# Threshold attention and a feed-forward block on one core: later weights, attention first on two engines, split scores from job three, a margin in the order

## The chip, the core and the metric

The kernel runs on one core of one Trainium2 chip. The metric is the device time of one execution in microseconds (us). The core has five engines that run side by side, each through its own list of instructions in order: PE (TensorE, the matrix multiplier; its weight loads are shown as PEld), DVE (VectorE), ACT (ScalarE), POOL (GpSimd) and SP (SyncE, which here issues every DMA). SBUF is the working memory, PSUM the memory that PE writes.

## The reference

For 8 batches, 8 heads, 576 positions and 64 values a head, attention keeps of each row of scores only those within `tau` of the row's largest, and takes a softmax over them. Its output, 8 x 576 x 512, goes through a feed-forward block (FFN) in which each position is mixed with the one before it, twice (`xk` and `xr`).

```python
scores = scale * np.matmul(q, k.transpose(0, 1, 3, 2))
thresh = np.max(scores, axis=-1, keepdims=True) - tau
scores = np.where(scores >= thresh, scores, -1000000000.0)
scores = scores - np.max(scores, axis=-1, keepdims=True)
attn = np.exp(scores)
attn = attn / (np.sum(attn, axis=-1, keepdims=True) + 1e-09)
x = np.matmul(attn, v)                    # then (B, S, H * D) = (8, 576, 512)
...
xk = mu_k * x + (1.0 - mu_k) * x_prev
xr = mu_r * x + (1.0 - mu_r) * x_prev
k = np.maximum(xk @ w_k, 0.0)             # w_k 512 x 1024
v = k * k @ w_v                           # w_v 1024 x 512
r = 1.0 / (1.0 + np.exp(-(xr @ w_r)))     # w_r 512 x 512
return (r * v).astype(np.float32)
```

The three weight matrices come as float64.

## The kernel before

**Planned order.** The program is not written in the order in which it runs. Each piece of work is a `Step`, added to a `Plan` with its engine, an estimate of how long it occupies it (`occ`), what it reads and writes, and a `key` (a small key goes first). `Plan.order` then goes through time with these estimates: it takes, over all engines, the step that could start first (ties by key), gives it its buffer, and so makes a list, in which the steps are issued. The chip runs each engine's part of this list in that order. So a changed estimate or key moves instructions on every engine. PSUM has two kinds of tile: `s` (two of them, scores of one head for 128 queries) and `w` (four, everything else).

**Jobs and units.** A job is a pair of heads of one batch; here jobs are counted from one. Most have five units: a tail `T` of 64 queries and four blocks `P` of 128 queries. Batch one is done in two halves, so that the first FFN chunk can start early: jobs one to four have two blocks each, jobs five to eight two blocks and the tail. A block has two halves `y`, one for each head.

**A block's way.** Scores on PE into `s` (L498 or L509); DVE takes the row maximum (L543); ACT shifts it by tau (L551) and takes the exponential into `p` (L559); DVE sets to zero what lies under the threshold and sums the row (L567), and inverts the sum (L577, L578); POOL scales the row (L592); PE transposes it in blocks of 128 (L617), ACT or DVE copies these from PSUM to `pm` and `pl` (L629, L631; DVE takes one of the two only where the block's number is above `EARLY`). After two blocks `attend` multiplies them with v (L690, L693), and DVE copies the result to `xT` (and the tail to `xE`).

**Two ways to score.** The first `PLAIN` = 8 jobs multiply in float32 straight from `raw` (L498), one step that fills both `s` tiles. The others split each operand into a high part `hi` (ACT, L422) and a rest `lo` (POOL, L428, two instructions a job), lay them out in `st` tiles by eight DMAs a job (L447; there are three pairs of `st` tiles, a job uses two), and score each half by a step of its own (L509, the tail L484).

**Weights.** The 20 weight tiles (8 of `w_k`, 4 of `w_r`, 8 of `w_v`) are fetched as 64-bit words (L331) and turned into numbers: ACT takes the absolute value of the high word (L340), DVE four steps (L348, L362, L369, L379), ACT makes the high part (L386), POOL the rest (L390). `xT` of the second batch serves as scratch for this. The plan lets the j-th fetch start at W0 + W1 * j = 3 + 3.5 j of its own time.

**FFN chunks.** A chunk is 256 positions: POOL takes the difference of neighbours (L777), DVE the mix (L786), ACT and POOL split it (L799, L807). Then PE multiplies with `w_k` (L829), ACT takes relu, square and high part (L837, L838, L842), POOL the rest (L852); PE multiplies with `w_r` (L871) and `w_v` (L893), each product as three matmuls of split operands; the sigmoid is ACT's (L879), the last product DVE's (L899). There are 18 chunks: two a batch, and one for the tails of every four batches. The first chunk needs jobs one to four. Steps of chunks may fill in anywhere behind their key.

## Time and profile before

| what | value |
| --- | --- |
| median of three runs | 1138.61 us (1138.51 to 1140.61) |
| the profiled execution | 1139.91 us, span of the profile 1137.8 us |
| busy, share of the span | PE 92%, DVE 68%, ACT 64%, POOL 49% |
| granted TensorE clock, mean | 0.968 |

A profile row gives line, engine, operation, out<-in by the program's names, partitions x elements, and the count. In groups, busy time and mean duration (ns) follow, then the idle time of that engine just before them and what ended most of it. Times of PE are modelled at their ends: matmuls overlap, so starts are what to read. A rise of one engine's busy time costs nothing where it is not waited for.

### The profile page before, as it was taken

To read this page: it belongs to the slowest core of one execution; us is meant where nothing else is said; L and a number is where in the kernel's file an instruction comes from. 1 tells how busy PE (TensorE), PEld (TensorE's weight loads), DVE (VectorE), ACT (ScalarE), POOL (GpSimd) and SP (SyncE) were. 2 spreads that over 40 slices of the span, in tenths; PEclk is the share of its full clock that TensorE was granted. 3 is DMA by queue.
4 is the path that set the end of the run, shared out by engine and by line. 5 is a ranking of instruction groups with operands and counts; after the bars stand their busy time and mean duration, and the time that the engine had idled before them with its cause. 6 is when DMAs were issued, how large, how long until landed. Compare 5 with 4: busy or idle time off the path is not lost.

```text
span 1137.8 us, 19250 instructions
## 1 busy us (share of the span) xinstructions
PE 1047.7 (92%) x6840; PEld 850.9 (75%) x6840; DVE 770.0 (68%) x1703; ACT 725.4 (64%) x1532; POOL 554.7 (49%) x570
## 2 busy tenths in 40 slices
PE   5557988997999999999999999999999999999998
PEld 3335757875878778787877878787787878688887
DVE  6999457778777777778767777778877677611120
ACT  5565677766777757677674767777576667444443
POOL 2656335634654536456444644545454544444441
PEclk8767998999999999999999999999999999999999
DMA  6530154445525336254523534344543341000000
GB/s 236 195 127 35 46 161 105 110 100 122 132 61 146 80 97 150 61 121 100 143 53 94 123 95 117 81 109 99 137 110 91 75 92 38 10 23 25 19 19 19
DMA packets 36798, 106.76 MB, mean 94 GB/s; under 512 B 5984, under 2 KB 5984, under 8 KB 36704
## 3 DMA queue, kind: packets, MB, share of 16 engines
q1 hardware_dynamic: 36704, 105.54, 36.1%
q8 instruction: 55, 0.90, 0.3%
q14 instruction: 39, 0.32, 0.1%
HBM read 44.70 MB, written 9.44 MB: 48 GB/s over the span
## 4 chain that ended last, share of the span: by engine, by line
PE 62%; DVE 20%; ACT 9%; POOL 3%; issue 3%; DMA 2%; SPq 1%; POOLq 0%; DVEq 0%; ACTq 0%
PE w L829 14%; PE w L893 11%; PE w L617 10%; PE s L509 8%; PE w L690 8%; PE w L871 6%; DVE p L567 5%; DVE mk L786 5%; DVE sm L543 3%; ACT p L559 2%; PE w L693 2%; DVE sm L577 2%; POOL p L592 2%; PE s L484 2%; PE s L498 1%
## 5 line engine op out<-in xcount | busy, mean ns | idle before, releaser
L592 POOL TENSOR_SCALAR p<-p,sm 128x576 f32<-128x576 f32 x288 | 220.9, 779 | 287.9 <-DVE sm L578 195.5
L567 DVE SCALAR_TENSOR_TENSOR p<-s,sm,p 128x576 f32<-128x576 f32 x288 | 232.5, 814 | 96.9 <-ACT p L559 93.6
L543 DVE TENSOR_REDUCE sm<-s 128x1 f32<-128x576 f32 x288 | 210.9, 751 | 47.3 <-PE s L509 29.2
L829 PE MATMUL w<-xk,wk 128*128 128x256 f32 x1728 | 235.0, 285 | 0.2 <-ACT pm L629 0.2
L617 PE MATMUL w<-ident,p 128*128 128x128 f32 x1312 | 200.8, 285 | 25.9 <-POOL p L592 23.2
L893 PE MATMUL w<-wv,k 128*128 128x512 f32 x864 | 221.4, 397 | 1.1 <-DVE sg L899 0.9
L829 PEld LDWEIGHTS w<-xk,wk 128*128 128x128 f32 x1728 | 218.1, 190 | 2.0 <-issue 0.8
L617 PEld LDWEIGHTS w<-ident,p 128*128 128x128 f32 x1312 | 153.6, 145 | 77.2 <-POOL p L592 54.6
L559 ACT ACTIVATE p<-s,sm 128x576 f32<-128x576 f32 x288 | 209.9, 732 | 0.5
L893 PEld LDWEIGHTS w<-wv,k 128*128 128x128 f32 x864 | 155.6, 188 | 30.1 <-issue 1.2
L629 ACT ACTIVATE pm<-w 128x512 f32<-128x512 f32 x178 | 105.2, 592 | 110.3 <-PE w L617 109.7
L551 ACT ACTIVATE sm<-sm,small 128x1 f32<-128x1 f32 x288 | 83.7, 291 | 108.1 <-DVE sm L543 106.7
L690 PE MATMUL w<-pm,v 128*64 128x256 f32 (+1 forms) x1024 | 146.8, 426 | 4.9 <-DVE pm L631 2.7
L852 POOL TENSOR_TENSOR k<-r,k 128x512 fp32r<-128x512 f32 x72 | 93.3, 1296 | 85.4 <-ACT k L842 79.8
L786 DVE SCALAR_TENSOR_TENSOR mk<-m,mu_sb,xT 128x256 f32<-128x256 f32 x128 | 79.6, 662 | 80.7 <-POOL xk L807 80.4
L807 POOL TENSOR_TENSOR xk<-mk,xk 128x512 fp32r<-128x512 f32 x72 | 93.3, 1296 | 70.0 <-ACT xk L799 66.7
L690 PEld LDWEIGHTS w<-pm,v 128*64 128x64 f32 x1024 | 74.8, 142 | 59.6 <-issue 11.1
L509 PE MATMUL s<-st 128*128 128x288 f32 x448 | 106.3, 319 | 13.9 <-DVE p L567 7.3
L871 PE MATMUL w<-wr,xk 128*128 128x512 f32 x432 | 111.4, 397 | 0.0
L428 POOL TENSOR_TENSOR lo<-raw,hi 128x576 fp32r<-128x576 f32 (+1 forms) x56 | 83.6, 1509 | 56.5 <-ACT hi L422 46.3
L509 PE MATMUL s<-st,st 128*128 128x288 f32 x448 | 99.4, 304 | 0.0
L509 PEld LDWEIGHTS s<-st 128*128 128x128 f32 x448 | 72.6, 193 | 34.7 <-issue 17.0
(62 smaller groups left out, 1140.9 us busy)
## 6 DMA issues: line engine op xcount, KB each, us to landing
raw<-in_qk SPq DMA_DIRECT2D x36, 608.0 KB, 4.8
st<-hi SPq DMA_DIRECT2D x56, 304.0 KB, 3.3
st<-lo SPq DMA_DIRECT2D x56, 304.0 KB, 4.3
v<-in_v SPq DMA_DIRECT2D x36, 320.0 KB, 3.0
out<-sg SPq DMA_DIRECT2D x32, 256.0 KB, 2.0
st<-hi SPq DMA_DIRECT2D x56, 144.0 KB, 3.4
st<-lo SPq DMA_DIRECT2D x56, 144.0 KB, 3.7
wk<-in_w_k SPq DMA_DIRECT2D x8, 512.0 KB, 7.1
```

What stands on the lines that cost most here:

```text
L509: PE.matmul(ss[y].get()[:, z, 0:HS], l.get()[:, c * P : (c + 1) * P], r.get()[:, keys(y, z)], start=(j == 0), stop=(j == 1),)
L543: lambda sv=sv, col=col: V.tensor_reduce(col(0), sv(), axis=AX.XY, op=ALU.max, negate=True),
L559: lambda sv=sv, pv=pv, col=col: A.activation(pv(), sv(), AF.Exp, bias=col(0)),
L567: lambda sv=sv, pv=pv, col=col: V.scalar_tensor_tensor(pv(), sv(), col(1), pv(), op0=ALU.is_ge, op1=ALU.mult, accum_out=col(2)),
L592: lambda y=y: G.tensor_scalar(p.get()[:, y], p.get()[:, y], sm.get()[:, 3, y : y + 1], 0.0, op0=ALU.mult, op1=ALU.add),
L617: lambda c=c, o=o: PE.transpose(pt.get()[:, c, :], p.get().rearrange("p y s -> p (y s)")[:, o : o + P], ident.get()),
L629: fn = lambda: A.activation(out_(), in_(), AF.Copy)
L690: PE.matmul(o.get()[hs, 0:n], vt.get()[:, c, hs], pm.get()[:, h, c, 0:n], start=(c == 0), stop=False)
L786: V.scalar_tensor_tensor(d.get()[:, y, o : o + n], diff.get()[:, y, o : o + n], mu_sb.get()[:, j, hc + y : hc + y + 1], prv[:, hc + y], op ...
L829: PE.matmul(h.get()[:, f], l, r, start=(ct == 0 and i == 0), stop=(ct == NCT - 1 and i == 2))
L871: PE.matmul(z.get(), l, r, start=(ct == 0 and i == 0), stop=(ct == NCT - 1 and i == 2))
L893: PE.matmul(vps.get(), l, r, start=(ft == 0 and i == 0), stop=(ft == NFT - 1 and i == 2))
```

## The change

- `w_r` and `w_v` may be fetched in the plan only from 50 + 2 (j - 8) on, for the j-th tile; `w_k` as before.
- `soft`: DVE's and ACT's steps of the weights and of FFN chunks stand back. In the choice among an engine's steps they count as if they could start 0.3 later; the engine may so be kept for a step of attention that is ready a little later.
- `LATE`: from 150 of the plan's time on, PE's attention steps (those with key under -500) count as ready 0.3 later than their inputs are.
- `PLAIN` is 2: jobs three to eight use split scores.
- `EARLY` is 16 instead of 40: from job five on DVE takes one of the two `pm` copies.
- the four transposes of a half are one step; `attend` of the first units is five steps, one for each block of keys; keys of early `attend` move by 4.5 instead of 1.5.
- a second buffer for `r` (relu), and other estimates for some steps.

```diff
-    HOP = 0.05
+    HOP, LATE, FROM = 0.05, 0.3, 150.0
+    SOFT = {"DVE": 0.3, "ACT": 0.3}
...
+        s.soft = self.SOFT.get(eng, 0.0) if self.soft else 0.0
...
-                    k = (t, s.key, i)
+                    k = (t + s.soft, s.key, i, t)
...
-                n.ready = max(n.ready, t + s.occ if same else s.end + self.HOP)
+                late = self.LATE if n.eng == "PE" and n.key < -500 and t > self.FROM else 0.0
+                n.ready = max(n.ready, t + s.occ if same else s.end + self.HOP + late)
...
-    PREP, PB, VB, COLD, EARLY = 6, 2, 2, 24, 40
+    W0, W1, W2, W3, AVK = 3.0, 3.5, 50.0, 2.0, 4.5
+    PREP, PB, VB, COLD, EARLY = 6, 2, 2, 24, 16
...
-            wait=W0 + W1 * j,
+            wait=wait,
...
-                        0.104,
+                        0.26,
...
-        for c, o in enumerate(at):
-            add(
-                "PE",
-                0.109,
...
+        occ = 0.109 * len(at)
+        add(
+            "PE",
+            occ,
+            mm,
+            reads=[*((p, z) for z in y), ident],
+            writes=[pt, *to],
...
-        occ = 10 * 0.842e-3 * n + 0.2
-        if key < COLD:
-            occ *= 2
...
+        early = key < EARLY
+        for j, cs in enumerate([[0], [1], [2], [3], [4]] if early else [range(5)]):
+            occ = len(cs) * 1.66e-3 * n * (2 if key < COLD else 1) + (0.1 if early else 0.35)
...
-            r = sbuf("r", [P, 512], F32, 1)
+            r = sbuf("r", [P, 512], F32, 2)
...
-    PLAIN = 8
+    PLAIN = 2
...
-    W0, W1 = 3.0, 3.5
+    wfr = [W0 + W1 * j if j < 8 else W2 + W3 * (j - 8) for j in range(len(wlist))]
...
-                    attend(job, g, unit["n"] + 1.5)
+                    attend(job, g, unit["n"] + (AVK if unit["n"] < 20 else 1.5))
```

What this does to the order is shown at three places. A row is line, operation, out<-in and shape, with the matmuls of one group merged (x4); the number after a name tells tiles apart. Line numbers of the new kernel are 6 to 20 higher.

DVE, around the fourth block (the second of job two). Before, from behind this block's two reductions to the first of the next block:

```order
L379 SCALAR_TENSOR_TENSOR xT_77<-wk_0_167,xT_77 128x512
L379 SCALAR_TENSOR_TENSOR xT_77<-wk_0_189,xT_77 128x512
L567 SCALAR_TENSOR_TENSOR p_292,sm_279<-s_257,sm_279,p_292 128x576
L567 SCALAR_TENSOR_TENSOR p_292,sm_279<-s_259,sm_279,p_292 128x576
L348 TENSOR_SCALAR xT_77<-xT_77 128x512
L577 TENSOR_SCALAR sm_279<-sm_279 128x2
L578 RECIPROCAL sm_279<-sm_279 128x2
L362 TENSOR_SCALAR xT_77<-xT_77 128x512
L348 TENSOR_SCALAR xT_77<-xT_77 128x512
L369 SCALAR_TENSOR_TENSOR xT_77<-wk_0_230,xT_77 128x512
L362 TENSOR_SCALAR xT_77<-xT_77 128x512
L543 TENSOR_REDUCE sm_323<-s_308 128x1
```

And now:

```order
L551 TENSOR_REDUCE sm_270<-s_248 128x1
L551 TENSOR_REDUCE sm_270<-s_250 128x1
L386 SCALAR_TENSOR_TENSOR xT_77<-wk_0_146,xT_77 128x512
L355 TENSOR_SCALAR xT_77<-xT_77 128x512
L575 SCALAR_TENSOR_TENSOR p_294,sm_270<-s_248,sm_270,p_294 128x576
L644 COPY xT_73<-w_222 128x256
L369 TENSOR_SCALAR xT_77<-xT_77 128x512
L551 TENSOR_REDUCE sm_311<-s_305 128x1
L575 SCALAR_TENSOR_TENSOR p_294,sm_270<-s_250,sm_270,p_294 128x576
L585 TENSOR_SCALAR sm_270<-sm_270 128x2
L586 RECIPROCAL sm_270<-sm_270 128x2
L575 SCALAR_TENSOR_TENSOR p_322,sm_311<-s_305,sm_311,p_322 128x576
```

`wk` are weight tiles, `xT_77` their scratch. Before, seven of the eleven steps between the reductions of this block and the next belong to weights; now three and a copy of `xT` stand there, and the first reduction of job three (`s_305`, split scores) stands ahead of the masking of this block's second half.

PE, where the first FFN matmul stands. Before:

```order
L498 MATMUL s_709<-raw_408 128x288
L498 MATMUL s_711<-raw_408 128x288
L498 MATMUL s_709<-raw_408 128x288
L498 MATMUL s_711<-raw_408 128x288
L617 MATMUL w_727<-ident,p_702 128x128 x4
L617 MATMUL w_734<-ident,p_702 128x128
L829 MATMUL w_736<-xk_428,wk_0_155 128x256 x3
L829 MATMUL w_736<-xk_428,wk_0_184 128x256 x3
L829 MATMUL w_736<-xk_428,wk_0_238 128x256 x3
L829 MATMUL w_736<-xk_428,wk_0_243 128x256 x3
L829 MATMUL w_736<-xk_428,wk_0_155 128x256 x3
L829 MATMUL w_736<-xk_428,wk_0_184 128x256 x3
```

And now:

```order
L517 MATMUL s_714<-st_2_514 128x288 x2
L517 MATMUL s_714<-st_2_514,st_2_520 128x288 x2
L624 MATMUL w_740<-ident,p_667 128x128 x4
L624 MATMUL w_747<-ident,p_667 128x128
L624 MATMUL w_764<-ident,p_730 128x128 x4
L624 MATMUL w_774<-ident,p_730 128x128 x4
L624 MATMUL w_782<-ident,p_730 128x128
L849 MATMUL w_786<-xk_522,wk_0_163 128x256 x3
L704 MATMUL w_791<-pm_708,v_543 64x320 x8
L704 MATMUL w_791<-pl_725,v_543 64x320 x2
L849 MATMUL w_786<-xk_522,wk_0_206 128x256 x3
L849 MATMUL w_786<-xk_522,wk_0_266 128x256 x3
```

The FFN's first product (`w_736`, `w_786`) stands behind the tail of job five before, and now behind that job's second block too, whose rows are `p_730`; job five's `attend` follows at once.

SP, from the fetch of job three's `raw` on. Before:

```order
L400 DMA raw_135<-in_qk 128x1216
L331 DMA wk_0_146<-in_w_k 128x512
L331 DMA wk_0_167<-in_w_k 128x512
L331 DMA wk_0_189<-in_w_k 128x512
L331 DMA wk_0_230<-in_w_k 128x512
L331 DMA wk_0_246<-in_w_k 128x512
L413 DMA v_254<-in_v 128x640
L400 DMA raw_276<-in_qk 128x1216
L331 DMA wr_0_284<-in_w_r 128x512
L331 DMA wr_0_303<-in_w_r 128x512
L331 DMA wr_0_328<-in_w_r 128x512
```

And now:

```order
L408 DMA raw_135<-in_qk 128x1216
L338 DMA wk_0_146<-in_w_k 128x512
L338 DMA wk_0_165<-in_w_k 128x512
L455 DMA st_0_183<-hi_177 64x1216
L455 DMA st_0_187<-hi_177 64x576
L455 DMA st_1_199<-hi_177 64x1216
L455 DMA st_1_212<-hi_177 64x576
L338 DMA wk_0_216<-in_w_k 128x512
L455 DMA st_0_187<-lo_195 64x576
L455 DMA st_1_212<-lo_195 64x576
L408 DMA raw_236<-in_qk 128x1216
L455 DMA st_0_183<-lo_195 64x1216
```

Five tiles of `w_k` were fetched in one go; now three of them stand behind transfers that wait for `hi` and `lo`, and `w_r` comes much later.

More of the change, by code (lines that the diff above doesn't have):

```diff
@@ L44 @@
         "eng", "occ", "lat", "fn", "key", "deps", "succ", "allocs", "idx", "missing", "ready",
-        "start", "end", "kb",
+        "start", "end", "kb", "soft",
     )
 class Plan:
-    HOP = 0.05
+    HOP, LATE, FROM = 0.05, 0.3, 150.0
+    SOFT = {"DVE": 0.3, "ACT": 0.3}
     def __init__(self):
@@ L58, in __init__ @@
         self.bufs = []
+        self.soft = False
     def buf(self, *a, **k):
@@ L167, in order @@
                 if pick is not None and (best is None or pick[0] < best[0]):
-                    best = (pick[0], e, pick[2])
+                    best = (pick[0], e, pick[2], pick[3])
             if best is None:
                 raise RuntimeError("the plan is stuck")
-            t, e, i = best
+            _, e, i, t = best
             s = steps[i]
@@ L315, in tile_threshold_attention_then_rwkv_ffn, with weight @@
     pieces = {}
-    def weight(j, name, w, c, f, key):
+    def weight(j, name, w, c, f, key, wait):
+        plan.soft = True
         tag = f"w{name}{c}{f}"
@@ L394, in weight @@
         )
+        plan.soft = False
     def operands(job, key):
@@ L612, in transposes, with mm @@
         pt = psum("w", [P, 4, P], 4)
-        for c, o in enumerate(at):
-            add(
-                "PE",
-                0.109,
-                lambda c=c, o=o: PE.transpose(
-                    pt.get()[:, c, :], p.get().rearrange("p y s -> p (y s)")[:, o : o + P], ident.get()
-                ),
-                reads=[*((p, z) for z in y), ident],
-                writes=[(pt, c), *(to if c == 0 else ())],
-                key=key - 1000,
-                lat=0.28,
-            )
+        def mm():
+            for c, o in enumerate(at):
+                PE.transpose(
+                    pt.get()[:, c, :], p.get().rearrange("p y s -> p (y s)")[:, o : o + P], ident.get()
+                )
+        occ = 0.109 * len(at)
[5 more added lines that the diff above has]
+            writes=[pt, *to],
+            key=key - 1000,
+            lat=occ + 0.18,
+        )
         return pt
@@ L668, in turn_last @@
                 "ACT",
-                0.13,
+                0.22,
                 pe,
@@ L683, in attend, with mm @@
         o = psum("w", [P, 512], 4)
-        def mm():
-            for c in range(4):
+        def mm(cs):
+            for c in cs:
                 for h in range(2):
                     hs = slice(h * D, (h + 1) * D)
-                    PE.matmul(o.get()[hs, 0:n], vt.get()[:, c, hs], pm.get()[:, h, c, 0:n], start=(c == 0), stop=False)
-            for h in range(2):
-                hs = slice(h * D, (h + 1) * D)
-                PE.matmul(o.get()[hs, 0:n], vt.get()[:, 4, hs], pl.get()[:, 0:n], start=False, stop=True)
-        occ = 10 * 0.842e-3 * n + 0.2
-        if key < COLD:
-            occ *= 2
-        free = [(x, (hp, g))] + ([(xE, (b % NE, hp))] if n > CH else [])
-        add("PE", occ, mm, reads=[vt, pm, pl], writes=[o, *free], key=key - 1000, lat=occ + 0.2)
+                    pt = pl.get() if c == 4 else pm.get()[:, h, c]
+                    PE.matmul(o.get()[hs, 0:n], vt.get()[:, c, hs], pt[:, 0:n], start=(c == 0), stop=(c == 4))
+        free = [(x, (hp, g))] + ([(xE, (b % NE, hp))] if n > CH else [])
+        early = key < EARLY
+        for j, cs in enumerate([[0], [1], [2], [3], [4]] if early else [range(5)]):
+            occ = len(cs) * 1.66e-3 * n * (2 if key < COLD else 1) + (0.1 if early else 0.35)
+            add(
+                "PE",
+                occ,
+                lambda cs=cs: mm(cs),
+                reads=[vt, pm, pl],
+                writes=[o, *(free if j == 0 else [])],
+                key=key - 1000,
+                lat=occ + 0.2,
+            )
         evict(
@@ L766, in ffn_chunk @@
         pool_tt = 1.17 if kind == "main" else NTB * 0.39
+        plan.soft = True
         mix = [sbuf("xk", [P, 2, NCT, CH], FR, 2) for _ in range(2)]
@@ L793, in scale @@
                             )
-                add("DVE", 0.7 if nseg == 1 else 1.04, scale, reads=[diff, mu_sb, *sr], writes=[d], key=key)
+                add("DVE", 0.8 if nseg == 1 else 1.57, scale, reads=[diff, mu_sb, *sr], writes=[d], key=key)
                 add(
@@ L913, in ffn_chunk @@
                 )
+        plan.soft = False
     halved = {0: ([0, 1], [2, "T", 3])}
-    PLAIN = 8
+    PLAIN = 2
     jobs = []
@@ L942, in tile_threshold_attention_then_rwkv_ffn @@
     for j, (name, w, c, f) in enumerate(wlist):
-        weight(j, name, w, c, f, wat[j])
+        weight(j, name, w, c, f, wat[j], wfr[j])
     for job in jobs:
```

## Prediction

> **What bounds the kernel now.** I read the busy time by stretches first. Columns: stretch, its length, then PE, weight loads, DVE, ACT and POOL busy (with instruction counts), granted clock, DMA share, GB/s.
>
> ```profile
> 0.00:105.00 105.00, 58.66 (x255) 37.88 (x255) 93.18 (x172) 58.94 (x115) 53.13 (x49) 0.76 0.43 155
> 105.00:181.00 76.00, 69.77 (x426) 51.23 (x425) 42.84 (x102) 51.28 (x111) 31.31 (x34) 0.95 0.37 103
> 181.00:300.00 119.00, 108.12 (x731) 86.94 (x733) 92.06 (x210) 81.41 (x183) 58.76 (x64) 0.96 0.44 105
> 300.00:1000.00 700.00, 677.94 (x4644) 556.41 (x4641) 517.99 (x1159) 477.78 (x1034) 357.95 (x377) 1.00 0.40 96
> 1000.00:1138.00 138.00, 133.18 (x793) 118.47 (x791) 23.92 (x64) 55.94 (x89) 53.51 (x49) 1.00 0.06 20
> ```
>
> The kernel has two regimes. Up to 105 us DVE is busy 93.2 of 105 us and TensorE only 58.7, at a clock of 0.76. From there on TensorE is the bound: it idles 6.2, 10.9, 22.1 and 4.8 us in the four later stretches, 44 in all, against 46 in the first 105. Then the timeline of TensorE, for the borders (start, duration, instruction):
>
> ```profile
> 104.87 4.61 PE L829 MATMUL w<-xk,wk 128*128 128x256 f32 x33
> ...
> 162.92 1.62 PE L893 MATMUL w<-wv,k 128*128 128x512 f32 x6
> ...
> 179.34 0.76 PE L617 MATMUL w<-ident,p 128*128 128x128 f32 x5
> ...
> 180.21 0.42 PE L509 MATMUL s<-st,st 128*128 128x288 f32 x2
> ```
>
> The first FFN matmul starts at 104.9: from here TensorE always has something to fill in. The first chunk ends at 164.5. The last two rows belong to job eight; I come back to them. Last, what DVE does before 105 (count, busy us, mean ns, idle before):
>
> ```profile
> L567 DVE SCALAR_TENSOR_TENSOR p<-s,sm,p 128x576 f32<-128x576 f32 x19 | 15.1, 813 | 2.0 <-ACT p L559 1.9
> L362 DVE TENSOR_SCALAR xT<-xT 128x512 uint32<-128x512 uint32 x20 | 13.8, 698 | 0.0
> L543 DVE TENSOR_REDUCE sm<-s 128x1 f32<-128x576 f32 x19 | 13.4, 745 | 6.1 <-PE s L498 6.1
> L348 DVE TENSOR_SCALAR xT<-xT 128x512 f32<-128x512 f32 x20 | 11.4, 584 | 0.0
> L369 DVE SCALAR_TENSOR_TENSOR xT<-wk,xT 128x512 uint32<-128x512 uint32 x8 | 7.5, 952 | 0.1
> L369 DVE SCALAR_TENSOR_TENSOR xT<-wv,xT 128x512 uint32<-128x512 uint32 x7 | 7.2, 1035 | 0.0
> L379 DVE SCALAR_TENSOR_TENSOR xT<-wv,xT 128x512 uint32<-128x512 uint32 x7 | 6.5, 933 | 0.0
> L379 DVE SCALAR_TENSOR_TENSOR xT<-wk,xT 128x512 uint32<-128x512 uint32 x8 | 5.4, 680 | 0.0
> L786 DVE SCALAR_TENSOR_TENSOR mk<-m,mu_sb,xT 128x256 f32<-128x256 f32 x8 | 4.8, 636 | 0.0
> L577 DVE TENSOR_SCALAR sm<-sm 128x2 f32<-128x2 f32 (+1 forms) x10 | 4.6, 462 | 0.0
> L369 DVE SCALAR_TENSOR_TENSOR xT<-wr,xT 128x512 uint32<-128x512 uint32 x4 | 4.0, 994 | 0.0
> L379 DVE SCALAR_TENSOR_TENSOR xT<-wr,xT 128x512 uint32<-128x512 uint32 x4 | 3.8, 950 | 0.0
> ```
>
> The eight weight rows (L348, L362, L369, L379) add to 59.6 us: decoding the weights is more than half of what bounds the first stage, and only w_k is needed for its end.
>
> **Stage one, to the first FFN matmul.** In the new order DVE has, ahead of the mix that releases this matmul, 10, 8, 8 and 8 of the four weight steps, all of w_k but two, where the trace has 20, 20, 19 and 19. At the means above 24.3 us stay (5.8, 5.6, 7.5, 5.4) and 35.3 go. But those means hold waiting; alone, the steps are short:
>
> ```profile
> 78.09 0.42 DVE L362 TENSOR_SCALAR xT<-xT 128x512 uint32<-128x512 uint32 x1
> ...
> 79.03 0.68 DVE L369 SCALAR_TENSOR_TENSOR xT<-wv,xT 128x512 uint32<-128x512 uint32 x1
> ```
>
> At these, 22 short and 22 long steps removed are 24.2 us. I take the middle, 29.7, since both kinds of row stand in the trace. Added are two reductions, two maskings and a small step (job five's second half now comes before the FFN's start): 3.6 us. So without new waits the stage ends at 104.9 - 29.7 + 3.6 = 78.8.
>
> New waits: jobs three to eight get split scores. The cost on TensorE is nothing:
>
> ```profile
> 76.97 1.24 PE L498 MATMUL s<-raw 64*128 64x288 f32 x8
> 82.82 3.04 PE L498 MATMUL s<-raw 64*128 64x288 f32 x8 [4.61 <-issue]
> ...
> 227.46 0.42 PE L509 MATMUL s<-st 128*128 128x288 f32 x2
> ...
> 228.51 1.54 PE L893 MATMUL w<-wv,k 128*128 128x512 f32 x6
> ```
>
> Plain scores of a unit take 1.24 us at full clock and 3.04 at the low one; the split ones 228.51 - 227.46 = 1.05, and each half needs only its own PSUM tile. The price is the operands: one ACT copy, two POOL subtractions and eight transfers for each job.
>
> ```profile
> L422 ACT ACTIVATE hi<-raw 128x1216 fp32r<-128x1216 f32 x6 | 7.3, 1221 | 4.1 <-PE s L484 2.5 <-DMA st<-lo 1.5
> L428 POOL TENSOR_TENSOR lo<-raw,hi 128x576 fp32r<-128x576 f32 (+1 forms) x12 | 17.7, 1491 | 11.4 <-ACT hi L422 11.4
> 156.85 3.24 SPq L447 DMA_DIRECT2D st<-lo  x4
> st<-lo SPq DMA_DIRECT2D x56, 304.0 KB, 4.3
> ```
>
> From a landed raw tile to a usable operand: 1.22 + 2 x 1.49 + some 6.5 for eight issues (twice 3.24) + 4.3 to land = 15 us. For later jobs it lies beside the job before. For job three it does not quite: its raw tile takes the place of job one's, so the chain starts when job one's last scores are done, and only job two lies beside it, two units of 3.6 us of DVE (two reductions, two maskings, a small step) with some weight steps between; I put 3 us there. On POOL the lo pair of job four stands ahead of job two's last softmax scaling: 3 us more, as DVE waits for nothing else it could do (in the new order a reduction of the next unit stands ahead of the rest of this one). The three late w_k fetches queue behind these transfers on SP too; they have until some 60 us, so I cost that at nothing. If every one of jobs three to six paid the pair, it would be 12, and with SP twice 18. So stage one ends at 78.8 + 6 = 85, bounds 73 (all 35.3 gone, no wait) and 102 (24.2 gone, 18 of waits).
>
> Here a rule speaks against the change. The row: POOL's softmax scaling has a mean of
>
> ```profile
> L592 POOL TENSOR_SCALAR p<-p,sm 128x576 f32<-128x576 f32 x19 | 21.7, 1152 | 26.0 <-DVE sm L578 25.0 <-PE s L498 1.0
> L592 POOL TENSOR_SCALAR p<-p,sm 128x576 f32<-128x576 f32 x58 | 42.8, 750 | 68.9 <-DVE sm L578 65.0 <-PE w L617 2.4 <-DVE sm L577 1.5
> ```
>
> 1152 ns before 105 us, beside weight steps, and 750 in 105 to 300. The Trainium skill (SBUF — State Buffer, section "SBUF: two separate sides") says that VectorE and GpSimd share one port pair as an exclusive lock, held for the whole instruction. The trace agrees in direction; by it the eight lo subtractions now in stage one would hold DVE for up to 8 x 1.49 = 11.9 us and the stage would end at 97, not 85. I do not take it whole, since reductions and maskings from PSUM, at 745 and 813 ns here, are not stretched.
>
> **Stage two, to the end of the first chunk.** The weights are not saved, they come here: 10, 12, 12 and 12 steps, 37.8 us at the means, 25.6 at the short rows. With 19 reductions (14.2), 17 maskings (13.8), ten small steps (4.6), six mixes (3.8) and seven of the PSUM copies, which the lower EARLY moves from ACT to DVE,
>
> ```profile
> L631 DVE COPY pm<-w 128x512 f32<-128x512 f32 x16 | 11.0, 688 | 6.8 <-PE w L617 6.6
> ```
>
> (4.8), DVE has 67 to 79 us of work, middle 73. At the end of that stage the new order has job eight done, job nine's tail transposed and its first unit and a half scored: the point that the trace reaches at 180.6, not 164.5 (rows at 179.34 and 180.21). TensorE needed 69.8 us for it from 105. So DVE bounds this stage as well, but with TensorE close behind; I take DVE's 73 times the slack that TensorE shows between 181 and 300 (119 / 108.1 = 1.10), 80 us, between 70 and 90. The stage ends at 165, against 180.6: 15.6 us gained. That, not the 35 us taken out of stage one, is what is left: it comes from filling DVE, which was busy 42.8 of 76 us after 105.
>
> **The rest.** From there TensorE has the same work. The 0.3 us margin can only take waits like these back (us in all, times, longest):
>
> ```profile
> PE w L617 <- POOL p L592: 7.5, 11, 1.4
> PE s L509 <- DVE p L567: 4.8, 10, 1.2
> ```
>
> 12.3 of the 22.1 us idle in 300 to 1000. Atomic transposes, corrected costs and the second relu buffer bring no instruction more or less; a new order may lose as well as win. I take a third, 4 us, between -8 and +12. The end changes little: 138 us of pure FFN stay.
>
> **Sum.** 15.6 + 4 = 19.6 off the profiled execution's 1139.9 (span 1137.8) is 1120.3; the median of the runs is 1.3 lower: 1119.
>
> **Rivals.**
> - Stage two stays full: w_v comes in between attention steps, the two accumulators of the first chunk hold two of four PSUM work tiles for most of it, and DVE needs its upper sum, 79 x 1.13 (the 105 / 93.2 of stage one) = 90 us. It ends at 175: 1129. For it: TensorE and DVE are both nearly full there. Against: DVE could be 93.2 of 105 us busy because weights were always ready to fill in; they are here too.
> - Slower: the shared port. Sixteen lo subtractions now fall in the two stages, four did before. If each of the twelve new ones stops DVE for its 1.49 us, that is 17.9; and if the weight steps in stage two stretch its 17 scalings from 750 to 1152 ns, 6.8 more: 24.7 us, 1144. It eats the gain from 17 us on, seven tenths of that price, and from 22 the kernel is slower. For it: 1152 against 750 ns. Against: half of DVE's work reads PSUM and keeps its time.
> - The margin works in full, 18 us over 181 to 1000 (12.3 scaled by 33 / 22.1 us of idle): 1105. Against: most waits are under 1.4 us but not under 0.3.
> - Nothing moves: the lead of attention is given back in later waits for the x tile, since FFN has to free it. Then 1139. For it: attention can be two batches ahead at most. Against: the TensorE work done early is done.
>
> **Chances.** Forecast 0.53 (own range 1110 to 1128), full stage two 0.20, margin 0.12, port 0.10, nothing 0.05. Within 0.2% (2.3 us, about what a measurement of this kernel tells from no change): 0.07, the last with a little of the second; slower 0.10, faster 0.83. The range leaves out the far end of the margin and most of the port: 1103 to 1137.
>
> **What would show it.** The first FFN matmul at 73 to 102 us, 85 forecast; if later, look on DVE for waits on scores, and on SP for st issues. The chunk's last w_v matmul at 165; past 175 the second rival holds, and PE waits there name DVE. L348 to L379 with means over 0.8 us beside more POOL work would speak for the port. In 300 to 1000, TensorE waits on POOL and DVE below 12 us would show the margin, above it that the order lost. Wrong altogether if stage one ends past 100.

## The result, and the profile after

| | median, us | runs, us | ratio to before, 95% interval |
|---|---|---|---|
| before | 1138.56 | 1137.66 to 1140.61 | |
| changed | 1119.79 | 1117.88 to 1123.23 | 0.9836 [0.9806, 0.9866] |
| changed, a second time | 1120.2 | 1117.19 to 1121.6 | 0.985 [0.9832, 0.9868] |

The kernel is 17 to 19 us faster; 1119.0 was forecast. The profiled execution took 1118.3 us, its span is 1116.5 against 1137.8 before: 21.3 us to account for. First the stretches, cut where the prediction cut them: at the first FFN matmul, at the first chunk's last w_v matmul, then at 300 and 1000 us. Columns: stretch, length, busy time (and count) of PE, weight loads, DVE, ACT and POOL, granted clock, DMA share, GB/s.

```profile
0.00:88.06 88.06, 56.48 (x262) 38.07 (x262) 69.88 (x137) 56.85 (x116) 48.84 (x48) 0.79 0.86 243
88.06:171.35 83.29, 69.16 (x408) 54.00 (x406) 75.97 (x138) 60.47 (x127) 56.03 (x47) 0.91 0.59 160
171.35:300.00 128.65, 117.41 (x812) 94.84 (x813) 105.80 (x234) 87.78 (x197) 66.00 (x70) 0.97 0.45 109
300.00:1000.00 700.00, 682.28 (x4681) 565.46 (x4678) 511.32 (x1149) 485.87 (x1034) 365.83 (x380) 1.00 0.39 95
1000.00:1116.50 116.50, 111.91 (x678) 100.06 (x676) 22.58 (x57) 45.07 (x72) 41.95 (x39) 1.00 0.07 21
```

The two border rows in the timeline of TensorE (start, duration, instruction):

```profile
88.06 0.99 PE L849 MATMUL w<-xk,wk 128*128 128x256 f32 x3
...
169.89 1.56 PE L913 MATMUL w<-wv,k 128*128 128x512 f32 x6
```

Stage one fell from 104.9 to 88.1 us, near the forecast of 85. Stage two is the stretch in which DVE is busy 76.0 of 83.3 us: the weight decoding did come here. Its end, 171.4, stands against 180.6 for the same state before, so 9.2 us are gained there, not 15.6. The rest then gave 12.1 us, not 4. **The total is right because two errors cancel, which is luck**, and the experiments look for the reason of each.

DVE's weight steps in stage one (five rows) and stage two (six rows): count, then busy us and mean ns, then idle before.

```profile
L376 DVE SCALAR_TENSOR_TENSOR xT<-wk,xT 128x512 uint32<-128x512 uint32 x8 | 8.0, 1007 | 0.1
L386 DVE SCALAR_TENSOR_TENSOR xT<-wk,xT 128x512 uint32<-128x512 uint32 x8 | 7.3, 916 | 0.0
L355 DVE TENSOR_SCALAR xT<-xT 128x512 f32<-128x512 f32 x10 | 7.3, 750 | 1.4 <-ACT xT L347 1.4
L369 DVE TENSOR_SCALAR xT<-xT 128x512 uint32<-128x512 uint32 x10 | 5.4, 553 | 0.0
...
L376 DVE SCALAR_TENSOR_TENSOR xT<-wr,xT 128x512 uint32<-128x512 uint32 x1 | 1.1, 1148 | 0.0
...
L386 DVE SCALAR_TENSOR_TENSOR xT<-wv,xT 128x512 uint32<-128x512 uint32 x8 | 10.1, 1261 | 0.1
L355 DVE TENSOR_SCALAR xT<-xT 128x512 f32<-128x512 f32 x10 | 8.5, 853 | 0.0
L369 DVE TENSOR_SCALAR xT<-xT 128x512 uint32<-128x512 uint32 x10 | 7.4, 742 | 0.0
L376 DVE SCALAR_TENSOR_TENSOR xT<-wv,xT 128x512 uint32<-128x512 uint32 x8 | 6.9, 865 | 0.1
...
L386 DVE SCALAR_TENSOR_TENSOR xT<-wr,xT 128x512 uint32<-128x512 uint32 x4 | 4.0, 1012 | 0.0
...
L376 DVE SCALAR_TENSOR_TENSOR xT<-wr,xT 128x512 uint32<-128x512 uint32 x3 | 2.0, 679 | 0.0
```

29.1 us in stage one and 38.9 in stage two, above the upper end of 25.6 to 37.8. The same 80 steps have become longer: w_v's second long step takes 1261 ns, where 933 stood in the prediction. Three of the 37 steps in stage one stand behind the mix that releases the first FFN matmul; the 34 ahead of it are those that the prediction counted. Last, TensorE's waits in 300 to 1000 us (total, times, longest):

```profile
PE s L517 <- issue: 6.1, 3, 2.1
PE w L624 <- POOL p L600: 3.8, 3, 1.6
PE s L517 <- DVE p L575: 3.4, 7, 0.9
```

The waits on POOL and DVE that the margin is aimed at went from 12.3 to 7.2 us. But a new row of 6.1 us stands above them.

### The profile page after: what moved, and what is told of

Same layout as the page of the kernel before. It is cut to its first block, busy times and chain, and to the rows that moved or that the text cites. A ratio compares the mean times of both kernels' runs of the same rounds, so it can differ in the third digit from the quotient of the medians.

```text
span 1116.5 us, 19374 instructions
## 1 busy us (share of the span) xinstructions
PE 1037.2 (93%) x6832; PEld 852.4 (76%) x6832; DVE 785.5 (70%) x1712; ACT 736.0 (66%) x1543; POOL 578.6 (52%) x582
## 4 chain that ended last, share of the span: by engine, by line
PE 73%; DVE 13%; ACT 6%; DMA 4%; issue 3%; POOL 1%; SPq 0%; POOLq 0%; ACTq 0%
PE w L913 16%; PE w L849 15%; PE w L704 11%; PE w L624 11%; PE s L517 10%; PE w L891 8%; DVE p L575 4%; PE s L492 2%; ACT p L567 2%; DVE sm L551 2%; DMA raw<-in_qk 1%; DVE sm L585 1%; DMA st<-lo 1%; DMA wk<-in_w_k 1%; DVE mk L806 1%
## 5 line engine op out<-in xcount | busy, mean ns | idle before, releaser
L600 POOL TENSOR_SCALAR p<-p,sm 128x576 f32<-128x576 f32 x288 | 225.5, 792 | 268.9 <-DVE sm L586 227.1
L849 PE MATMUL w<-xk,wk 128*128 128x256 f32 x1728 | 231.0, 284 | 0.0
L624 PE MATMUL w<-ident,p 128*128 128x128 f32 x1312 | 197.0, 285 | 19.8 <-POOL p L600 14.8
L642 ACT ACTIVATE pm<-w 128x512 f32<-128x512 f32 x169 | 99.7, 593 | 98.2 <-PE w L624 96.8
L806 DVE SCALAR_TENSOR_TENSOR mk<-m,mu_sb,xT 128x256 f32<-128x256 f32 x128 | 88.6, 732 | 83.5 <-POOL xk L827 83.4
L517 PE MATMUL s<-st 128*128 128x288 f32 x496 | 119.1, 322 | 27.3 <-DVE p L575 11.7
L559 ACT ACTIVATE sm<-sm,small 128x1 f32<-128x1 f32 x288 | 83.5, 290 | 83.4 <-DVE sm L551 80.3
L704 PEld LDWEIGHTS w<-pm,v 128*64 128x64 f32 x1024 | 71.6, 141 | 64.1 <-issue 10.3
L517 PEld LDWEIGHTS s<-st 128*128 128x128 f32 x496 | 79.7, 193 | 51.4 <-issue 29.0
L436 POOL TENSOR_TENSOR lo<-raw,hi 128x576 fp32r<-128x576 f32 x68 | 102.1, 1518 | 31.2 <-ACT hi L430 23.7
L517 PE MATMUL s<-st,st 128*128 128x288 f32 x496 | 110.6, 305 | 0.0
```

The lines of the kernel that those rows point to most:

```text
L436: lambda cs=cs: G.tensor_tensor(lo.get()[:, cs], raw.get()[:, cs], hi.get()[:, cs].bitcast(F32), op=ALU.subtract),
L517: PE.matmul(ss[y].get()[:, z, 0:HS], l.get()[:, c * P : (c + 1) * P], r.get()[:, keys(y, z)], start=(j == 0), stop=(j == 1),)
L600: lambda y=y: G.tensor_scalar(p.get()[:, y], p.get()[:, y], sm.get()[:, 3, y : y + 1], 0.0, op0=ALU.mult, op1=ALU.add),
L624: PE.transpose(pt.get()[:, c, :], p.get().rearrange("p y s -> p (y s)")[:, o : o + P], ident.get())
L704: PE.matmul(o.get()[hs, 0:n], vt.get()[:, c, hs], pt[:, 0:n], start=(c == 0), stop=(c == 4))
L806: V.scalar_tensor_tensor(d.get()[:, y, o : o + n], diff.get()[:, y, o : o + n], mu_sb.get()[:, j, hc + y : hc + y + 1], prv[:, hc + y], op ...
```

## The experiments

Ratios are against the kernel before on the same chip. The change itself was run again beside them, since its first interval is wide:

> The changed kernel once more, unedited, so that the edits to it can be read against a ratio with a narrower interval than 0.9806 to 0.9866. If 0.983 to 0.985 comes out, leaving out the margin (0.9844) did nothing, and plain scores for eight jobs (0.9812) are some 3 us better than the change; if 0.981 to 0.982, they are the same and the margin helps by 3 us.

It came out at 0.985, the first of these two cases. This table is what the traces give for each kernel: the first FFN matmul; the start of the last 6171 matmuls (by count, which is the end of the first chunk in before and in the change); the time from there to the last matmul and TensorE's idle in it; and how many stretches of 3.41 us at half the granted clock fall into it. How a span splits at that point is good to some us only, since an order may put wide matmuls on either side. The row of the change has the second ratio and the first trace; its second trace has 89.8, 171.7, 942.1, 28.8 and 3. Where a kernel is compared with the change below, the first ratio, 0.9836, would make a gain 1.6 us smaller and a loss 1.6 us larger. A trace is one execution: those of e2, e3 and e9 are the longest of their runs, 2 to 3 us over the median.

| kernel | ratio, 95% interval | first FFN | to the last 6171 | rest | idle in it | half clock |
|---|---|---|---|---|---|---|
| before | | 104.9 | 179.7 | 953.5 | 33.0 | 4 |
| changed | 0.985 [0.9832, 0.9868] | 88.1 | 169.9 | 942.0 | 29.0 | 3 |
| e1 no margin | 0.9844 [0.983, 0.9857] | 89.0 | 170.6 | 941.4 | 22.2 | 4 |
| e2 early fetch | 0.989 [0.9876, 0.9903] | 83.4 | 184.2 | 935.4 | 24.3 | 2 |
| e3 plain scores, 8 jobs | 0.9812 [0.9791, 0.9832] | 90.4 | 172.6 | 939.4 | 26.0 | 3 |
| e4 no standing back | 0.9861 [0.9848, 0.9875] | 88.8 | 180.8 | 933.9 | 24.5 | 2 |
| e6 before, atomic transposes | 0.9995 [0.9984, 1.0006] | 105.5 | 179.1 | 949.8 | 30.9 | 4 |
| e7 before, late fetch | 0.9901 [0.9885, 0.9917] | 96.1 | 172.5 | 946.4 | 31.6 | 1 |
| e8 old costs | 0.9805 [0.979, 0.982] | 85.0 | 171.2 | 937.2 | 27.5 | 1 |
| e9 before, atomic, standing back | 0.9785 [0.977, 0.98] | 97.9 | 170.8 | 939.0 | 25.4 | 3 |
| e10 one relu buffer | 0.9807 [0.979, 0.9825] | 88.0 | 174.6 | 933.3 | 20.6 | 4 |
| e11 plain scores and old costs | 0.9741 [0.9727, 0.9754] | 90.0 | 166.5 | 936.5 | 25.1 | 1 |

### One part of the change undone

**e1: no margin.**

```diff
-    HOP, LATE, FROM = 0.05, 0.3, 150.0
+    HOP, LATE, FROM = 0.05, 0.0, 150.0
```

> The changed kernel with the 0.3 us margin ahead of attention's TensorE steps set to 0; all else stays. Up to 150 us the order is the same, so the first FFN matmul stays at 88. Theory A (the early stages give 9 us; of the 12 us that the rest gave, only the 4 us less idle are the margin's, the 8 us of shorter TensorE time come from the atomic transposes and the corrected costs): 1124 us, 4 over the changed kernel, and TensorE waits on POOL and DVE between 300 and 1000 go from 7 back towards 12 us. Rival B (the margin makes the whole 12 us, since it also groups matmuls of one kind): 1131 or more. Rival C (the margin does nothing, the new order of the rest is due to other parts): 1119 to 1121.

The ratio is that of the change: rival C. Its waits in 300 to 1000:

```profile
PE w L624 <- POOL p L600: 6.0, 7, 1.9
PE s L517 <- DVE p L575: 4.6, 11, 1.0
```

10.6 us on POOL and DVE against 7.2 with the margin, so the margin does what it says to these waits, and the time does not change. The 6.1 us of "issue" are gone here, and TensorE idles less in the rest (22.2 against 29.0 us). In this trace the margin took waits from one row and put them into another.

**e2: early fetch.**

```diff
-    wfr = [W0 + W1 * j if j < 8 else W2 + W3 * (j - 8) for j in range(len(wlist))]
+    wfr = [W0 + W1 * j for j in range(len(wlist))]
```

> The changed kernel with w_r and w_v fetched at the old times (3 + 3.5 j us in the planner) again; all else stays. Theory A (DVE bounds stage one, and decoding w_r and w_v there is what held up the first FFN matmul): this matmul moves from 88 back to 98 to 105, the end of the first chunk from 171 to some 178, and the time goes to 1126 to 1129. Rival D (split scores and the standing back of weight steps do it alone, since a step with the margin of 0.3 us lets attention go ahead anyway): first FFN matmul stays within 3 us of 88 and the time within 2 us of 1119.8.

4.6 us slower than the change by the ratios (0.989 - 0.985, of 1138), short of the 6 to 9 of theory A, and not by its mechanism. The first FFN matmul comes earlier, not later:

```profile
83.38 0.87 PE L849 MATMUL w<-xk,wk 128*128 128x256 f32 x6
```

So with the other parts in place it isn't the late fetch that frees DVE for attention in stage one. The loss comes in stage two: the last 6171 matmuls begin at 184.2 instead of 169.9. Both theories fell: A on the first matmul, D on the time and, by 1.7 us, on the matmul too.

**e3: plain scores for eight jobs.**

```diff
-    PLAIN = 2
+    PLAIN = 8
```

> The changed kernel with plain scores for the first eight jobs again, as before; all else stays. My prediction put 6 us of waits on the split scores in stage one (3 for job three's operand, 3 on POOL), and saw no gain in them but TensorE time. Theory A (their price is real and their gain on TensorE lies beside DVE): the first FFN matmul comes 3 to 6 us earlier, at 82 to 85, and the time goes down by up to 3 us. Rival E (the split pays: at the low clock TensorE is late for the reductions, 3.04 us against about 1 us for a unit): first FFN matmul 3 to 10 us later than 88, time up by 3 to 8 us.

4.3 us faster than the change by the ratios (0.985 - 0.9812, of 1138), more than theory A's 3, though the two intervals touch at 0.9832. The first FFN matmul is 2 us later, not earlier, so the price of the split scores is not where I put it, in waits for operands ahead of this matmul. What did change is the rows of the weight steps, 0 to 171.35 us:

```profile
L369 DVE TENSOR_SCALAR xT<-xT 128x512 uint32<-128x512 uint32 x20 | 13.9, 711 | 0.1
L355 DVE TENSOR_SCALAR xT<-xT 128x512 f32<-128x512 f32 x20 | 9.1, 473 | 0.0
L386 DVE SCALAR_TENSOR_TENSOR xT<-wk,xT 128x512 uint32<-128x512 uint32 x8 | 7.5, 932 | 0.0
L386 DVE SCALAR_TENSOR_TENSOR xT<-wv,xT 128x512 uint32<-128x512 uint32 x8 | 7.3, 927 | 0.0
L376 DVE SCALAR_TENSOR_TENSOR xT<-wv,xT 128x512 uint32<-128x512 uint32 x8 | 6.9, 887 | 0.0
L376 DVE SCALAR_TENSOR_TENSOR xT<-wk,xT 128x512 uint32<-128x512 uint32 x8 | 6.7, 846 | 0.1
L376 DVE SCALAR_TENSOR_TENSOR xT<-wr,xT 128x512 uint32<-128x512 uint32 x4 | 4.5, 1116 | 0.0
...
L386 DVE SCALAR_TENSOR_TENSOR xT<-wr,xT 128x512 uint32<-128x512 uint32 x4 | 2.7, 677 | 0.0
```

58.6 us for the 80 steps; in the change they take 29.1 + 38.9 = 68.0. Here POOL does 4 lo subtractions before 171 us, there 16. e12 tests what such a meeting costs by itself; the single steps of the two traces say how often it happens. I put each of the 80 steps down to the POOL instruction that overlaps it longest. "Longer by" is against the steps that overlap none (0.42 us for a short one, 0.68 for a long one):

| | beside no POOL work | beside a scaling, longer by | beside a subtraction, longer by |
|---|---|---|---|
| changed | 22 | 27, 0.18 us each | 31, 0.64 us each |
| e3 | 19 | 51, 0.18 us each | 10, 0.65 us each |

Two long steps of the changed kernel, one clear of POOL and one behind a lo subtraction (DVE and POOL timelines):

```profile
138.99 0.69 DVE L386 SCALAR_TENSOR_TENSOR xT<-wv,xT 128x512 uint32<-128x512 uint32 x1
...
149.82 2.94 POOL L436 TENSOR_TENSOR lo<-raw,hi 128x576 fp32r<-128x576 f32 x2 [1.99 <-issue]
...
151.40 1.92 DVE L386 SCALAR_TENSOR_TENSOR xT<-wv,xT 128x512 uint32<-128x512 uint32 x1
```

But only five of the 31 steps are put down to a lo subtraction, 3.7 us in all; 18 are put down to the weights' own rests (L397), against six in e3. So most of the difference is the order, which puts weight steps beside other subtractions, and not a price of each added one, though the added ones may have shifted the others.

Nor is it shown that the shorter steps make e3 faster. Its trace, the longest of four runs, has a span of 1116.6 us against the change's 1116.5, and the last 6171 matmuls start 2.7 us later. The runs go from 1118.6 us at a mean granted clock of 0.974 to 1112.2 at 0.985, so the gain may go with the clock. What makes it stays open.

**e4: no standing back.**

```diff
-    SOFT = {"DVE": 0.3, "ACT": 0.3}
+    SOFT = {"DVE": 0.0, "ACT": 0.0}
```

> The changed kernel with weight and mix steps no longer standing back by 0.3 us on DVE and ACT; all else stays. Theory A (what counts early is when w_r and w_v are fetched; with those gone the remaining weight steps only fill gaps): the time stays within 2 us of 1119.8, first FFN matmul at 86 to 92. Rival F (the standing back is what lets attention run ahead, and it also sets the order of FFN's mixes later): time up by 4 us or more, with more TensorE waits on DVE between 171 and 1000.

1.3 us slower than the change by the ratios, and the intervals overlap, as theory A said. As with e2 the first FFN matmul is no later to speak of, stage two is 10 us longer, and the rest gives most of that back. Taken out of the whole, neither the fetch nor the standing back is worth much. That doesn't say that they do nothing; e7 and e9 ask it the other way round.

**e8: the planner's old costs.** No instruction more or less.

```diff
-                        0.26,
+                        0.104,
...
-                0.22,
+                0.13,
...
-            occ = len(cs) * 1.66e-3 * n * (2 if key < COLD else 1) + (0.1 if early else 0.35)
+            occ = len(cs) * 1.684e-3 * n * (2 if key < COLD else 1) + (0.04 if early else 0.2)
...
-                add("DVE", 0.8 if nseg == 1 else 1.57, scale, reads=[diff, mu_sb, *sr], writes=[d], key=key)
+                add("DVE", 0.7 if nseg == 1 else 1.04, scale, reads=[diff, mu_sb, *sr], writes=[d], key=key)
```

> The changed kernel with the planner's costs of before: bd copies 0.104, pl copies 0.13, attention matmuls 8.4 us per 1000 columns + 0.2 (ten matmuls), mix scalings 0.7 and 1.04 us. No instruction more or less, only the order that the planner finds. Theory A2 (the 12 us after the first chunk are the atomic transposes): within 3 us of the changed kernel. Rival G (they are the corrected costs, by which the planner no longer sends TensorE to steps whose operands are late): 1124 to 1131, with more of TensorE's waits on POOL and DVE between 300 and 1000 than 7.2 us.

Outside both: 0.9805, 5 us faster than the change. The corrected costs make the kernel slower.

**e10: one relu buffer.**

```diff
-            r = sbuf("r", [P, 512], F32, 2)
+            r = sbuf("r", [P, 512], F32, 1)
```

> The changed kernel with one relu buffer instead of two; all else stays. My prediction put the second buffer at nothing. Theory A: within 2 us of the changed kernel (1120). Rival J (ACT's relu waits on the square's and the multiplication's reads of the one buffer, and with it the PSUM tiles that TensorE needs, above all in the 138 us of pure FFN at the end): 1123 to 1127, most of it lost after 960 us.

Outside both again: 0.9807, 5 us faster. The first FFN matmul stays at 88.0, and in the pure FFN after 1000 us TensorE is busy all the time, so rival J's wait isn't there:

```profile
1000.00:1107.00 107.00, 107.00 (x647) 95.86 (x646) 18.42 (x53) 44.52 (x72) 41.91 (x39) 1.00 0.05 18
```

The rest has 20.6 us of idle instead of 29.0. A second buffer gives the planner more choices, and here it used them for a slower order. Why e8 and e10 are faster I can say only so far: less idle in the rest (e10), fewer stretches at half the clock (e8, one instead of three). Which decision of the planner causes it stays open.

### One part alone, in the kernel before

**e6: atomic transposes.** The four transposes of a half are one step.

```diff
-        for c, o in enumerate(at):
-            add(
-                "PE",
-                0.109,
-                lambda c=c, o=o: PE.transpose(
+        def mm():
+            for c, o in enumerate(at):
+                PE.transpose(
...
+        occ = 0.109 * len(at)
+        add(
+            "PE",
+            occ,
+            mm,
...
+            lat=occ + 0.18,
+        )
```

> The kernel before with one thing of the change: the four transposes of a half are one step of the plan, so that no other matmul comes between them; nothing else. After the first chunk the change needs 8 us less of TensorE's own time for the same 6171 matmuls and 4 us less idle, and the transposes carry most of it (169.0 to 162.6 us busy, idle before them 13.7 to 8.3). Theory A2 (leaving out the margin did not cost these 12 us, so the atomic transposes make them): 1126 to 1130 us, first FFN matmul as before at 104 to 106. Rival G (the corrected costs, the second relu buffer or a luckier order make it): 1134 to 1140.

Nothing that can be measured: theory A2 fell, though its evidence (shorter transposes in the changed trace) was true. The group of the transposes in the rest, before and in the change:

```profile
L617 PE MATMUL w<-ident,p 128*128 128x128 f32 x1143 | 169.0, 278 | 13.7 <-POOL p L592 11.2 <-DVE sg L899 1.0
L624 PE MATMUL w<-ident,p 128*128 128x128 f32 x1143 | 162.6, 275 | 8.3 <-POOL p L600 4.8 <-DVE xE L644 3.0 <-DVE pm L644 0.2
```

In e6 the group takes 169.2 us (1147 transposes), before, over the same count, 169.6. So the transposes got shorter with the order, not by the merging. The trace of e6 is 4.3 us shorter than that of before, at a ratio of 0.9995: differences of this size between two traces need not be the kernel's.

**e7: late fetch.**

```diff
-            wait=W0 + W1 * j,
+            wait=W0 + W1 * j if j < 8 else 50.0 + 2.0 * (j - 8),
```

> The kernel before with one thing of the change: w_r and w_v fetched from 50 us of the plan on, 2 us apart, instead of from 31 on, 3.5 apart; nothing else. Theory A (decoding w_r and w_v is what fills DVE ahead of the first FFN matmul): this matmul moves from 104.9 to 90 to 97, and the time goes down by 4 to 9 us, to 1129 to 1134. Rival D (early fetching in the changed kernel cost 4 us and left the first FFN matmul at 83, so what moved it is attention's lead over the weight steps, not the fetch): first FFN matmul within 4 us of 105, time within 3 us of before.

Theory A's step holds here, by more than it said in the time: first FFN matmul at 96.1, time down by 11.3 us.

```profile
96.08 1.65 PE L829 MATMUL w<-xk,wk 128*128 128x256 f32 x6
```

**e9: standing back,** with the atomic transposes of e6, since with single ones the planner gets stuck. The flag is set at the start of `weight` and in `ffn_chunk` ahead of the mixes, and taken back at their ends.

```diff
+    SOFT = {"DVE": 0.3, "ACT": 0.3}
...
-                    k = (t, s.key, i)
+                    k = (t + s.soft, s.key, i, t)
...
+        plan.soft = True
...
+        plan.soft = False
```

> The kernel before with two things of the change: the atomic transposes (alone: ratio 0.9995), and weight and mix steps that stand back by 0.3 us on DVE and ACT; the fetches stay as before. In the changed kernel the early fetch cost only 4 us, while the late fetch alone made the kernel before 12 us faster. Theory A3 (both do the same thing, letting attention's DVE steps go ahead of the decoding of w_r and w_v, so that either is enough): first FFN matmul at 85 to 97, time 1123 to 1130. Rival H (they are independent, and the 4 us are all that the fetch is worth once other parts are there): first FFN matmul at 100 or later, time 1132 to 1138.

**0.9785: 24.5 us, more than the whole change.** The transposes alone give nothing, so it is the standing back, or the two together, which no run separates. By the first FFN matmul, at 97.9, one would not have guessed it. The stretches, cut as for the change:

```profile
0.00:88.06 88.06, 52.93 (x228) 34.19 (x228) 75.01 (x142) 50.07 (x99) 41.01 (x40) 0.77 0.50 183
88.06:171.35 83.29, 74.63 (x448) 52.68 (x447) 61.52 (x129) 58.79 (x125) 43.43 (x41) 0.94 0.32 91
171.35:300.00 128.65, 117.77 (x836) 96.76 (x834) 103.22 (x232) 92.98 (x209) 69.40 (x74) 0.97 0.49 117
```

In the second stretch DVE is busy 61.5 us against the change's 76.0, TensorE 74.6 against 69.2. The end of the first chunk comes at the same time, 170.8 against 169.9, though TensorE began FFN 10 us later: the change buys an early start and pays it back in stage two. The rest is 10.8 us shorter than in e6, 5.5 of it less idle; there it is the FFN's mixes that stand back, as the weights are done, though no run tried these alone. Theory A3's figures were missed, by 0.9 us in the first FFN matmul and by 10 in the time; its idea, that either rule is enough, fits e2, e4, e7 and e9.

### Two edits together

**e11: plain scores for eight jobs and the old costs** (the diffs of e3 and e8).

> The changed kernel with both edits that made it faster: plain scores for eight jobs (0.9812) and the planner's old costs (0.9805), against 0.985 for the change. If each takes away a loss of its own: 1110 us (4 + 5 off 1120). If both only dodge the same thing (stretches of 3.4 us at half the clock, behind TensorE's idle gaps in 100 to 300 us; the change has seven such after its first FFN matmul, these two five and six): 1114 to 1117.

1109.08 us, the fastest of all: 0.9741, 12.4 us below the change by the ratios. This is the first of the two cases: each takes away a loss of its own. The sum of both is 9.4 (4.3 + 5.1), and the 3 us more lie within the intervals of the ratios. Against e8 it is 7.3 us faster, clear of both intervals, so plain scores do help here. How they do is not separated: e11 has shorter weight steps than e8 (60.9 against 67.5 us, single rows added) and also a higher granted clock in the first 171.35 us (0.92 against 0.86).

### The shared port by itself

**e12** runs the disputed instructions alone.

> Not the layer at all: DVE does 12 short weight steps, 12 long ones (both from SBUF, 128x512) and 12 maximum reductions from PSUM, once alone, once beside a stream of POOL subtractions of 128x512, once beside POOL's scalings of 128x576; the output is a copied tile. This measures the disputed price of the shared port. By the lock of the Trainium skill (SBUF — State Buffer, section SBUF: two separate sides) the DVE steps from SBUF would alternate with the POOL instructions, each DVE step taking its own time plus most of a POOL instruction, some 1.2 to 1.9 us, and the reductions from PSUM would keep their 0.75 us. By the trace as I read it: short steps 0.42 alone and 0.5 to 0.8 beside POOL, reductions unchanged.

The timeline of DVE and POOL: each row is twelve DVE instructions; first alone, then beside subtractions on POOL (row L290), then beside scalings (row L294).

```profile
5.02 4.11 DVE L282 TENSOR_SCALAR o<-src 128x512 uint32<-128x512 uint32 x12
9.04 7.31 DVE L284 SCALAR_TENSOR_TENSOR o<-src,two 128x512 uint32<-128x512 uint32 x12
16.27 7.27 DVE L286 TENSOR_REDUCE cols<-acc 128x1 f32<-128x512 f32 x12
...
25.17 42.94 POOL L290 TENSOR_TENSOR g<-two,src 128x512 fp32r<-128x512 f32 x29
25.25 16.87 DVE L282 TENSOR_SCALAR o<-src 128x512 uint32<-128x512 uint32 x12 [1.38 <-POOL g L290]
42.04 20.08 DVE L284 SCALAR_TENSOR_TENSOR o<-src,two 128x512 uint32<-128x512 uint32 x12
62.04 7.25 DVE L286 TENSOR_REDUCE cols<-acc 128x1 f32<-128x512 f32 x12
...
69.58 6.44 DVE L282 TENSOR_SCALAR o<-src 128x512 uint32<-128x512 uint32 x12
69.76 36.99 POOL L294 TENSOR_SCALAR p<-p,sc 128x576 f32<-128x576 f32 x40 [1.65 <-DVE p L300]
75.94 10.09 DVE L284 SCALAR_TENSOR_TENSOR o<-src,two 128x512 uint32<-128x512 uint32 x12
85.95 7.25 DVE L286 TENSOR_REDUCE cols<-acc 128x1 f32<-128x512 f32 x12
```

A short weight step takes 4.11 / 12 = 0.34 us alone, 1.41 beside subtractions and 0.54 beside scalings; a long one 0.61, 1.67 and 0.84; a reduction from PSUM 0.61, 0.60 and 0.60. Beside a POOL subtraction each DVE step from SBUF pays 1.06 us more, and a reduction pays nothing. The single rows alternate one to one: one subtraction, one step. Beside scalings only every second step pays, 0.47 us. The Trainium skill (SBUF — State Buffer, section "SBUF: two separate sides") describes a lock that is held for the whole instruction. The trace agrees that the two engines exclude each other, but a step pays less than a whole POOL instruction, 1.06 and 0.47 us: beside reductions a subtraction starts every 1.22 us and a scaling every 0.72. My expectation of 0.5 to 0.8 us for a short step, read from means of a trace where POOL was mostly scaling or idle, fits the scalings (0.54) and was wrong for the subtractions (1.41).

## Why the prediction was right, and where it was not

- **Stage one, 85 forecast, 88.1 measured: the terms were right, the adding was not.** The sum took 29.7 of 59.6 us of weight steps out, so it left 29.9; 29.1 stayed. DVE's other rows grew by 3.6 us, as forecast (43.4 to 47.0), and its idle time by 6.4 (11.8 to 18.2), forecast 6. But rows of the profile overlap: before, 103.0 us of DVE rows are 93.1 us of busy time, and now 76.1 are 69.9. So 26.9 us less of rows gave only 23.2 less of busy time, and that is where the miss of 3 us lies. The waits on job three's operands came to 1.05 and 1.63 us (the second is put down to a w_k transfer), forecast 3.
- **What let attention go ahead** is not the late fetch alone: without it the first FFN matmul came at 83.4 (e2), without the standing back at 88.8 (e4). Either is enough, or nearly so; the prediction credited only the weights that come later.
- **Stage two, 80 forecast, 83.3 measured, by luck so close.** DVE's rows add to 83.1 us where the forecast had 73: the weight steps are 38.9, not 31.7, and the other rows 44.2, not 41.2. The overlap of rows takes 7.1 of that back, so DVE is busy 76.0 us, and the factor of 1.10 for its slack came out right. The weight steps are longer because more of them run beside POOL subtractions (the table under e3). Together these two stages gave 9.2 us where I said 15.6; the end at 171.4 lies between my 165 and the 175 of the rival "full stage two".
- **The port rival** had the right mechanism and counted the wrong thing. I set it aside because half of DVE's work reads PSUM. That work does keep its time: in the change, up to 171 us, a reduction takes 0.75 us both beside a POOL subtraction and beside no POOL work, a masking 0.81 in both, and a 128x512 copy 0.69 and 0.68. The weight steps read SBUF and pay. But the rival charged 1.49 us for each of twelve new lo subtractions, 17.9 in all; five weight steps are put down to a lo subtraction, for 3.7 us. In all, single rows added, the 80 steps take 6.0 us more than before (62.6 to 68.6), with 31 of them beside a subtraction instead of 23. The prediction charged its forecast with nothing for this. With the lock taken whole it had 97 us for stage one; 88 came.
- **The rest, 4 forecast, 12.1 measured, and from another part.** "The 0.3 us margin can only take waits like these back" was right about the waits (12.3 to 7.2 us) and wrong about the time: e1 shows the margin at nothing. The prediction priced the standing back in the early stages and nowhere else; in e9, added to the atomic transposes, it makes the rest 10.8 us shorter. But e4, without it, has a short rest too (933.9), so other parts do the same, and none of the parts that were taken out makes the rest longer. `EARLY`, the five steps of `attend`, their keys and the atomic transposes were not taken out of the change. Which decision of the planner it is stays open.
- **"TensorE has the same work" from there** holds by count, 6171 matmuls, not by time: 920.5 us without the idle before, 913.1 after. 1.7 us are one stretch less at half the clock; the rest is in how matmuls follow each other (the transposes' group fell from 169.0 to 162.6 us). Merging them alone has 918.9 in its one trace (e6).
- **"Corrected costs and the second relu buffer bring no instruction more or less"** is true and was taken for a price of nothing. By the ratios each costs about 5 us (e8, e10). With the split scores (4.3 us, and 7.3 between e8 and e11) the change carries three parts that make it slower, under one that is worth more than the total.
- **The parts don't add.** Late fetch alone 11.3 us, standing back with atomic transposes 24.5; but either taken out of the change costs only 1 to 5 us.

## What to carry to other kernels

When a planner orders the work, take each rule out and put each in alone: a rule worth 24 us on its own, with the step that it needs, looked worth 1 us when removed; that another rule covered for it fits the runs here. A stage's first matmul is a poor marker of progress; compare the point at which the same work is left. Before adding an elementwise operation on POOL, count the operations that DVE runs from SBUF beside it and charge each meeting, not each operation (here 1.06 us by itself, about 0.64 in the layer for a subtraction, 0.2 for a scaling); DVE's reductions, maskings and copies from PSUM kept their time. And rows of a profile can overlap: compare a sum of rows with the busy time before it is taken as time.

## What the runs showed of the hardware

From 200 us on the granted clock falls to half for 3.41 us at a time (6.83 once each in e1, e6 and e10), and a gap of about 2 us in TensorE's work can be enough. The changed kernel's timeline, with the idle time before the matmul in brackets, and then the granted clock (eighth column) in stretches of it:

```profile
273.01 2.82 PE L704 MATMUL w<-pm,v 128*64 128x256 f32 x13 [2.91 <-DVE pm L644]
...
789.67 0.50 PE L517 MATMUL s<-st 128*128 128x288 f32 x2 [2.04 <-issue]
```

```profile
218.90:222.30 3.40, 3.40 (x17) 2.42 (x18) 2.67 (x7) 0.92 (x2) 0.74 (x1) 0.50 0.89 254
273.50:276.90 3.40, 3.40 (x16) 1.68 (x12) 1.16 (x6) 0.00 (x0) 1.97 (x2) 0.50 0.88 255
```

```profile
785.00:800.00 15.00, 12.96 (x96) 10.75 (x95) 13.45 (x28) 9.08 (x25) 5.84 (x7) 1.00 0.53 142
```

The gap of 2.91 us is followed by a stretch at 0.50, the one of 2.04 us at 787 is not. Over the thirteen profiles of this layer (two of them of the same kernel), from 200 us to the last matmul, every such stretch has 1.6 to 2.9 us of TensorE idle in the four us ahead of it; of 31 gaps of 1.9 us or more, 21 were followed by one. So, as an estimate, such a gap costs itself and, two times in three, 1.7 us more (half of 3.41, where TensorE is the bound). The Trainium skill (TensorE: Matmul & The Clock Gate, section "HAM oscillation — how this bites in real kernels") gives idle gaps of over some 3.4 us as what to avoid; in these traces shorter ones count. The fastest kernel, e11, has no gap over 1.75 us after 200 us and no such stretch there.
